# Two projection tiles and one pool of four tiles in the key phase of a linear-attention kernel with an MLP behind it

## The chip, the cores and the metric

The kernel runs on one core of one Trainium2 chip. The core has five engines with queues of their own: TensorE (PE, with its weight loads shown as PEld), VectorE (DVE), ScalarE (ACT), GpSimd (POOL) and SyncE (SP), which here issues all DMAs. The metric is the device time of one execution in microseconds (us). Before the change three runs took 1204.83, 1207.55 and 1209.04 us; the median is 1207.55 us.

## The reference

The inputs are q, k and v of 8 batches, 8 heads, 576 tokens and 64 dimensions, a feature matrix w_phi of 64x128, and the two matrices of an MLP. Everything is float32.

```python
def phi(x):
    proj = np.einsum('bhsd,df->bhsf', x, w_phi)
    proj = proj - np.max(np.abs(proj), axis=-1, keepdims=True)
    return np.concatenate([np.exp(proj), np.exp(-proj)], axis=-1)
q_p, k_p = (phi(q), phi(k))
kv = np.einsum('bhsf,bhsd->bhfd', k_p, v)
z = np.sum(k_p, axis=2)
num = np.einsum('bhsf,bhfd->bhsd', q_p, kv)
den = np.einsum('bhsf,bhf->bhs', q_p, z)[..., None] + 1e-06
return (num / den).astype(np.float32)
...
h = x @ w_in
g = np.maximum(0.01 * h, h)
return (g @ w_out).astype(np.float32)
```

The second part takes the attention output, reordered to 4608 tokens of 512 features, through w_in (512x2048) and w_out (2048x512).

## The kernel before

**Attention.** The 64 pairs of batch and head are taken two heads at a time: 32 phases i, four per batch. A key phase, k_phase(i), builds kv and z of its two heads; a query phase, q_phase(i), uses them and writes the divided result into a ring that holds two batches. Phases 0 to 3 have their own code (first_k_phase, first_q_phase) and run at the start.

**Key phase.** 576 tokens are five chunks (four of 128 and one of 64) in three groups (2, 2 and 1 chunks). For each group the projection goes from PE into a PSUM tile of tag "a", is copied by ACT and added to by DVE into `pmk` (lines 244 to 249), and DVE takes its maximum into `m4` and the negative into `m4n` (lines 252 to 256). For each chunk ACT writes four exponentials into `ek` (lines 269, 270); ACT or DVE rounds it to `kph` (helper line 67 or 69); POOL or DVE subtracts to get the remainder `kpl` (helper line 72); and PE accumulates kph and kpl against the values into a PSUM tile of tag "c" (line 224). The last chunk keeps both halves in one tile (line 289). Then the sum is copied to `kvs`, transposed (line 301) and written as `kvh` and `kvl` (lines 311 to 314). Tiles of one name share a fixed number of places: ek 1, pmk 1, kph 2, kpl 1, m4 2; "a" has 3 places, "c" has 1. A tile waits until its place is free.

**Phases below 8** ("nat") multiply in plain float32 with `bd`, two copies of w_phi on a block diagonal (lines 342, 237). **From phase 8 on** operands are split into a rounded part and a remainder, and the projections use `wq` (lines 244, 344, 345), the split of w_phi, which split_w_phi makes at the start (lines 149 to 154).

**Query phase.** Four projections into tag "a", each transposed by DVE into `tq` (line 346), a maximum into `m` (line 348), three small DMAs to bring partitions together (line 350), a second maximum `mx` (line 353), three small DMAs back (line 355), subtraction (line 361), transpose into `mb` (line 363), exponentials `eq` (lines 368, 369), rounded part `qh` (line 375) and remainder `ql` (helper line 72, POOL), matmuls with kvh and kvl (lines 384 to 389) in tag "a", copies into the ring and `dn` (lines 391, 392) and the division.

**Order.** attention() takes one step (up to a yield) of k_phase(i) and one of q_phase(i-1) in turn. All attention work has a higher priority than the MLP's; a planner turns priorities and dependencies into one fixed order for each engine, which then runs as written.

**MLP.** 18 blocks of 256 tokens. split() makes `xh` and `xl` of a block from the ring; layer1 (lines 571 to 578) and layer2 (lines 591 to 593) run for 16 steps, with `gh` and `gl` in between. Block 2 needs attention batch 1 (phases 4 to 7), block 4 needs batch 2 (phases 8 to 11), block 6 needs batch 3 (phases 12 to 15). Weights are unpacked at the start through a scratch tile that shares the place of `kvl` (line 178). The output of a block goes through tile `o` to a DMA.

Of the kernel before, what the change touches and what calls it, by code (L numbers as in the profile page):

```python
# [17 lines left out]
P = 128  # L18
# [14 lines left out]
BUFS = {"kph": 2, "eq": 2, "m4": 2, "g": 2, "gh": 2, "gl": 2, "qh": 2, "ql": 2, "dn": 2}  # L33
# [11 lines left out]
def attention_moe_kernel(ctx: ExitStack, tc: tile.TileContext, q, k, v, vt, w_phi, w_in, w_out, out):  # L45
# [8 lines left out]
    def st(shape, dt, tag):  # L54
        return sp.tile(shape, dt, tag=tag, name=tag, bufs=BUFS.get(tag, 1))

# [35 lines left out]
    wq = ct([P, 2, F], F32R, "wq")  # L92
    wq_h, wq_l = wq[:, 0], wq[:, 1]
    bd = ct([P, 2 * F], F32, "bd")
# [53 lines left out]

    def split_w_phi():
        for j in range(2):  # L150
            r = slice(64 * j, 64 * j + 64)
            w = bd[r, F * j : F * j + F]
            nc.scalar.copy(wq_h[r], w)
            nc.vector.tensor_tensor(wq_l[r], w, wq_h[r].bitcast(F32), op=ALU.subtract)
# [50 lines left out]
    def k_phase(i):  # L205
# [14 lines left out]
        yield  # L220
        kvp = pt("c")
# [5 lines left out]
        for g in range(3):  # L227
# [4 lines left out]
            pmk = st([P, 4, F], F32, "pmk")  # L232
            if nat:
# [19 lines left out]
            mb = m4[r, 0 : 2 * w].unsqueeze(2).broadcast_to([n, 2 * w, F])  # L253
            if not nat:
                m4n = st([P, 4], F32, "m4n")
                nc.vector.tensor_scalar(m4n[r, 0 : 2 * w], m4[r, 0 : 2 * w], -1.0, None, op0=ALU.mult)
            if nat:
                nc.vector.tensor_tensor(pmk[r, 0 : 2 * w], pkv, mb, op=ALU.subtract)
            yield
            for s in range(w):  # L260
                c = 2 * g + s
                ek = st([P, 2, 256], F32, ("ek", "kph", "kpl")[c % 3] if nat else "ek")
                if nat:
                    nc.scalar.activation(ek[r, :, 0:F], pmk[r, 2 * s : 2 * s + 2], AF.Exp)
                    nc.scalar.activation(ek[r, :, F:256], pmk[r, 2 * s : 2 * s + 2], AF.Exp, scale=-1.0)
                else:
                    for j in range(2):
                        h = 2 * s + j
                        nc.scalar.activation(ek[r, j, 0:F], pmk[r, h], AF.Exp, bias=m4n[r, h : h + 1])  # L269
                        nc.scalar.activation(ek[r, j, F:256], pmk[r, h], AF.Exp, scale=-1.0, bias=m4[r, h : h + 1])  # L270
                if nat:
                    for j in range(2):
                        kv_mm(j, rv[r, 4 * j + c if c < 4 else 8 + j], ek[r, j], first=c == 0, last=c == 4)
                    yield
                    continue
                if c < 4:
                    kph = st([P, 2, 256], F32R, "kph")
                    kpl = st([P, 2, 256], F32R, "kpl")
                    copy_("kph", kph, ek)
                    tt_("kpl", kpl, ek, kph.bitcast(F32), ALU.subtract)  # L280
                    for j in range(2):
                        kv_mm(j, vh[:, 4 * j + c], kph[:, j], first=c == 0)
                        kv_mm(j, vl[:, 4 * j + c], kph[:, j])
                    for j in range(2):
                        kv_mm(j, vh[:, 4 * j + c], kpl[:, j])
                else:
                    kst = st([P, 2, 256], F32R, "kph")
                    copy_("kst", kst[r], ek[r])
                    nc.vector.tensor_tensor(kst[0:64], ek[r], kst[r].bitcast(F32), op=ALU.subtract)
                    for j in range(2):  # L290
                        kv_mm(j, vl[:, 8 + j], kst[:, j])
                        kv_mm(j, vh[:, 8 + j], kst[:, j], last=True)
                yield
        kvs = st([P, 2, 256], F32, "ek").rearrange("p a (b f) -> p a b f", b=2)[0:66]
# [26 lines left out]
    def q_phase(i):  # L321
# [11 lines left out]
        yield  # L333
        tq = st([P, 2, 2, U], F32, "tq")
        m = st([P, 4, 2, 18], F32, "m")
# [75 lines left out]
    def first_k_phase(i):  # L411
# [6 lines left out]
        for g in range(3):  # L418
# [10 lines left out]
            pm = st([P, 4, F], F32, ("kpl" if g % 2 else "kph") if od else ("ek" if g % 2 else "pmk"))  # L429
# [14 lines left out]
        kvs = st([P, 2, 256], F32, "kph").rearrange("p a (b f) -> p a b f", b=2)[0:66]  # L444
# [28 lines left out]
    def first_q_phase(u):  # L473
# [7 lines left out]
        for hp in range(1 if tail else NP):  # L481
# [6 lines left out]
            pm = st([P, 4, F], F32, "ek" if hp % 2 else "pmk")  # L488
# [49 lines left out]
    def attention():  # L538
        for i in range(NP, B * NP + 1):
            gens = [k_phase(i)] if i < B * NP else []  # L540
            if i > NP:
                gens.append(q_phase(i - 1))
            while gens:
                for it in list(gens):
                    if next(it, end) is end:
                        gens.remove(it)
                    else:
                        yield i - 1
            yield i
# [33 lines left out]
    def layer2(i, ft, half=range(TT)):  # L583
# [10 lines left out]
        if ft == NFT - 1:  # L594
            for t in half:
                o = st([P, DM], F32, "ek" if i == NBLK - 1 and t else "o")
                copy_("o", o, accs[i, t])
                r = i * T + t * P
                nc.sync.dma_start(out[r : r + P, :], o)
# [27 lines left out]
    split_w_phi()  # L627
# [60 lines left out]
```

## Time and profile before

| | |
|---|---|
| three runs, median (range) | 1207.55 us (1204.83 to 1209.04) |
| the profiled execution, its time | 1207.22 us |
| the profiled execution, its span | 1205.4 us |
| busy ACT, DVE, POOL | 861.8, 747.7, 631.5 us |
| mean granted clock of TensorE | 0.992 |

The span counts from the first to the last instruction that the profile shows. A busy time is the union of an engine's instructions; matmuls overlap, and their ends are modelled, so a busy PE is not yet a PE at its peak. In the slices of the span the engines look like this (each digit is the share of a slice of about 30 us in tenths):

```profile
PE   8899999899998999899999999999999999999998
DVE  5979984566767675766677666767876767510000
ACT  5977875778787787777787877778777788543232
POOL 0042222456566676666666666656566766453232
```

Until about 210 us the start phases, the weights and the nat phases run; then attention and MLP run side by side; from about 1070 us only the MLP is left. A row of the groups gives line, engine, operation, tiles, shapes and count, then busy us and mean ns; idle time before it and what ended it stand last. The chain of work is followed back from the end, each piece to what released it.

### The profile page before, as it was taken

What the parts mean: (1) busy time and instruction counts of PE and PEld (TensorE: products, weight loads), DVE (VectorE), ACT (ScalarE), POOL (GpSimd) and SP (SyncE); (2) the same over time, 40 slices, a digit from 0 to 9 for tenths busy, and PEclk for the clock granted to TensorE, in tenths of its full rate; (3) what the DMA queues carried; (4) which work ended last, traced back from release to release, by engine and by line L of the source; (5) the groups of instructions that cost most, each with busy time, mean ns of one, the idle gap of its engine ahead of it and who ended that gap; (6) DMA issues with size and microseconds to landing.
All of it is one profiled execution on the core that took longest, in us unless ns stands there. A gap on an engine that the chain in (4) does not pass through costs nothing.

```text
span 1205.4 us, 21633 instructions
## 1 busy us (share of the span) xinstructions
PE 1168.8 (97%) x7496; PEld 1035.9 (86%) x7496; DVE 747.7 (62%) x1327; ACT 861.8 (71%) x2267; POOL 631.5 (52%) x709
## 2 busy tenths in 40 slices
PE   8899999899998999899999999999999999999998
PEld 5577778699997999799998999899989999989997
DVE  5979984566767675766677666767876767510000
ACT  5977875778787787777787877778777788543232
POOL 0042222456566676666666666656566766453232
PEclk9999999899998999899999999999999999999999
DMA  7425241201111011111111011111011110000000
GB/s 215 142 81 167 88 116 32 77 23 33 50 32 48 18 44 33 50 24 32 50 32 40 22 50 33 40 33 50 21 40 32 41 33 19 3 18 5 14 18 18
DMA packets 70846, 57.82 MB, mean 48 GB/s; under 512 B 53201, under 2 KB 54353, under 8 KB 70737
## 3 DMA queue, kind: packets, MB, share of 16 engines
q1 hardware_dynamic: 70736, 56.44, 16.6%
q8 instruction: 59, 0.97, 0.3%
q14 instruction: 51, 0.41, 0.1%
HBM read 46.20 MB, written 9.44 MB: 46 GB/s over the span
## 4 chain that ended last, share of the span: by engine, by line
PE 69%; DVE 10%; ACT 9%; issue 4%; DMA 4%; SPq 2%; POOL 2%; DVEq 0%; POOLq 0%; ACTq 0%
PE h L571 9%; PE h L574 9%; PE h L572 9%; PE acc L591 8%; PE acc L592 8%; PE acc L593 8%; PE c L224 5%; PE a L384 2%; DMA mx<-mx 2%; PE a L244 2%; PE a L389 2%; PE a L386 2%; DMA m<-m 2%; DVE tq L361 1%; SPq L350 1%
## 5 line engine op out<-in xcount | busy, mean ns | idle before, releaser
L72 POOL TENSOR_TENSOR gl<-g,gh 128x256 fp32r<-128x256 f32 x288 | 231.3, 806 | 327.9 <-ACT gh L67 259.9
L571 PE MATMUL h<-xh,w0h 128*128 128x256 f32 x1088 | 281.1, 285 | 4.4 <-ACT g L578 2.4
L572 PE MATMUL h<-xh,w0l 128*128 128x256 f32 x1088 | 277.5, 282 | 0.0
L571 PEld LDWEIGHTS h<-xh,w0h 128*128 128x128 f32 x1088 | 205.9, 189 | 18.3 <-ACT g L578 4.2
L591 PE MATMUL acc<-w1h,gh 128*128 128x512 f32 x544 | 215.3, 396 | 0.7 <-DVE o L69 0.4
L592 PE MATMUL acc<-w1l,gh 128*128 128x512 f32 x544 | 214.8, 395 | 0.0
L572 PEld LDWEIGHTS h<-xh,w0l 128*128 128x128 f32 x1088 | 205.8, 189 | 8.9
L593 PE MATMUL acc<-w1h,gl 128*128 128x512 f32 x544 | 203.4, 395 | 0.7 <-POOL gl L72 0.7
L578 ACT ACTIVATE g<-h 128x256 f32<-128x256 f32 x288 | 109.1, 381 | 110.4 <-PE h L574 85.4
L574 PE MATMUL h<-xl,w0h 128*128 128x256 f32 x1088 | 187.4, 281 | 0.0
L72 POOL TENSOR_TENSOR ql<-eq,qh 128x576 fp32r<-128x576 f32 x96 | 148.8, 1569 | 53.6 <-DVE qh L375 31.7
L67 ACT CAST gh<-g 128x256 fp32r<-128x256 f32 x288 | 114.8, 403 | 57.5 <-PE acc L592 55.1
L574 PEld LDWEIGHTS h<-xl,w0h 128*128 128x128 f32 x1088 | 154.6, 188 | 0.6 <-POOL xl L72 0.2
L72 POOL TENSOR_TENSOR kpl<-ek,kph 128x512 fp32r<-128x512 f32 x72 | 98.4, 1366 | 37.4 <-ACT kph L67 14.5
L591 PEld LDWEIGHTS acc<-w1h,gh 128*128 128x128 f32 x544 | 102.4, 188 | 14.1 <-DVE o L69 0.7
L593 PEld LDWEIGHTS acc<-w1h,gl 128*128 128x128 f32 x544 | 99.1, 188 | 17.6 <-POOL gl L72 0.9
L592 PEld LDWEIGHTS acc<-w1l,gh 128*128 128x128 f32 x544 | 102.3, 188 | 12.6
L361 DVE TENSOR_TENSOR tq<-tq,mx 128x576 f32<-128x576 f32 x56 | 59.2, 1097 | 80.3 <-DMA mx<-mx 80.3
L269 ACT ACTIVATE ek<-pmk,m4n 128x128 f32<-128x128 f32 (+1 forms) x240 | 89.8, 393 | 16.1 <-POOL kpl L72 12.6
L375 DVE TENSOR_REDUCE qh<-eq 128x576 fp32r<-128x576 f32 x96 | 70.8, 749 | 44.4 <-ACT eq L369 20.2
L270 ACT ACTIVATE ek<-pmk,m 128x128 f32<-128x128 f32 (+1 forms) x240 | 89.1, 390 | 8.6 <-DVE m L252 8.1
L368 ACT ACTIVATE eq<-mb 128x288 f32<-128x288 f32 x112 | 49.2, 439 | 53.5 <-DVE mb L363 50.1
(202 smaller groups left out, 2363.9 us busy)
## 6 DMA issues: line engine op xcount, KB each, us to landing
out_dram<-o SPq DMA_DIRECT2D x35, 256.0 KB, 2.0
rq<-in_q_dram SPq DMA_DIRECT2D x28, 288.0 KB, 3.0
rk<-in_k_dram SPq DMA_DIRECT2D x27, 288.0 KB, 2.8
rv<-in_v_dram SPq DMA_DIRECT2D x29, 256.0 KB, 3.6
ring<-in_w_in_dram SPq DMA_DIRECT2D x9, 512.0 KB, 3.8
f<-in_w_out_dram SPq DMA_DIRECT2D x7, 512.0 KB, 3.6
f<-in_w_in_dram SPq DMA_DIRECT2D x7, 512.0 KB, 3.7
ring<-in_w_out_dram SPq DMA_DIRECT2D x5, 512.0 KB, 3.8
```

The lines of the kernel that those rows point to most:

```text
L67: nc.scalar.copy(o, i)
L72: (nc.vector if pick(key) == "v" else nc.gpsimd).tensor_tensor(o, a, b, op=op)
L269: nc.scalar.activation(ek[r, j, 0:F], pmk[r, h], AF.Exp, bias=m4n[r, h : h + 1])
L270: nc.scalar.activation(ek[r, j, F:256], pmk[r, h], AF.Exp, scale=-1.0, bias=m4[r, h : h + 1])
L361: nc.vector.tensor_tensor(tu, tu, mx[:, u].unsqueeze(2).broadcast_to([P, 18, 32]), op=ALU.subtract)
L571: nc.tensor.matmul(ph, lhsT=weight(0, "h", ft)[:, d * P : d * P + P], rhs=xh[d], start=d == 0, stop=False)
L572: nc.tensor.matmul(ph, lhsT=weight(0, "l", ft)[:, d * P : d * P + P], rhs=xh[d], start=False, stop=False)
L574: nc.tensor.matmul(ph, lhsT=weight(0, "h", ft)[:, d * P : d * P + P], rhs=xl[d], start=False, stop=d == NP - 1)
L578: nc.scalar.activation(g, ph, AF.Prelu, alpha=0.01)
L591: nc.tensor.matmul(a, lhsT=gh[:, ts], rhs=weight(1, "h", ft), start=ft == 0, stop=False)
L592: nc.tensor.matmul(a, lhsT=gh[:, ts], rhs=weight(1, "l", ft), start=False, stop=False)
L593: nc.tensor.matmul(a, lhsT=gl[:, ts], rhs=weight(1, "h", ft), start=False, stop=ft == NFT - 1)
```

## The change

The tiles ek, kph, kpl and kvs of the key phase get one common tag "kk" with four places (before 1 + 2 + 1). pmk gets two places, m4 three and m4n two. k_phase is cut into head(g), the projection and maximum of a group, and chunk(c); the program order becomes head 0, chunk 0, head 1, chunk 1, head 2, chunks 2 to 4, where it was head 0, chunks 0 and 1, head 1, chunks 2 and 3, head 2, chunk 4. The arithmetic is the same.

The places come from three others: wq now takes the place of bd, so it is made when phase 8 first asks for it (w_phi_split), from a second load of w_phi into the place of kvl; the query's m takes the place of mb. In attention(), q_phase(7) is taken five steps ahead of k_phase(8), since it is the last to read bd.

```diff
@@ -30,7 +30,7 @@
 NK = 8
-BUFS = {"kph": 2, "eq": 2, "m4": 2, "g": 2, "gh": 2, "gl": 2, "qh": 2, "ql": 2, "dn": 2}
+BUFS = {"kk": 4, "pmk": 2, "eq": 2, "m4": 3, "m4n": 2, "g": 2, "gh": 2, "gl": 2, "qh": 2, "ql": 2, "dn": 2}
 PBUFS = {"a": 3, "c": 1, "h": 2, "acc": 2}
@@ -51,8 +51,8 @@
 
-    def st(shape, dt, tag):
-        return sp.tile(shape, dt, tag=tag, name=tag, bufs=BUFS.get(tag, 1))
+    def st(shape, dt, tag, name=None):
+        return sp.tile(shape, dt, tag=tag, name=name or tag, bufs=BUFS.get(tag, 1))
 
@@ -89,9 +89,19 @@
     xl = ct([P, NP, T], F32R, "xl")
-    wq = ct([P, 2, F], F32R, "wq")
-    wq_h, wq_l = wq[:, 0], wq[:, 1]
-    bd = ct([P, 2 * F], F32, "bd")
+    bd = cp.tile([P, 2 * F], F32, tag="bd", name="bd", bufs=1)
+    split_w = {}
+
+    def w_phi_split():
+        if not split_w:
+            raw = st([P, F], F32, "kvl", "wr")
+            for j in range(2):
+                nc.sync.dma_start(raw[64 * j : 64 * j + 64], w_phi)
+            split_w[0] = w = cp.tile([P, 2, F], F32R, tag="bd", name="wq", bufs=1)
+            nc.scalar.copy(w[:, 0], raw)
+            nc.vector.tensor_tensor(w[:, 1], raw, w[:, 0].bitcast(F32), op=ALU.subtract)
+        return split_w[0]
+
     xbh = [st([P, 2, U], F32R, "qh")[:, :, 0:T] for _ in range(2)]
@@ -145,13 +155,6 @@
         first_load_v(i)
-
-    def split_w_phi():
-        for j in range(2):
-            r = slice(64 * j, 64 * j + 64)
-            w = bd[r, F * j : F * j + F]
-            nc.scalar.copy(wq_h[r], w)
-            nc.vector.tensor_tensor(wq_l[r], w, wq_h[r].bitcast(F32), op=ALU.subtract)
 
@@ -218,18 +221,22 @@
         yield
+        wq = None if nat else w_phi_split()
         kvp = pt("c")
...
 
-        for g in range(3):
+        heads = {}
+
+        def head(g):
             w = 2 if g < 2 else 1
...
             pmk = st([P, 4, F], F32, "pmk")
+            m4n = None
             if nat:
@@ -250,48 +257,58 @@
             nc.vector.tensor_reduce(m4[r, 0 : 2 * w], pkv, axis=AX.X, op=ALU.max, apply_absolute_value=True)
-            mb = m4[r, 0 : 2 * w].unsqueeze(2).broadcast_to([n, 2 * w, F])
-            if not nat:
+            if nat:
+                mb = m4[r, 0 : 2 * w].unsqueeze(2).broadcast_to([n, 2 * w, F])
+                nc.vector.tensor_tensor(pmk[r, 0 : 2 * w], pkv, mb, op=ALU.subtract)
+            else:
                 m4n = st([P, 4], F32, "m4n")
                 nc.vector.tensor_scalar(m4n[r, 0 : 2 * w], m4[r, 0 : 2 * w], -1.0, None, op0=ALU.mult)
+            heads[g] = r, pmk, m4, m4n
+            yield
+
+        def chunk(c):
+            g, s = divmod(c, 2)
+            r, pmk, m4, m4n = heads[g]
+            ek = st([P, 2, 256], F32, "kk", "ek")
             if nat:
-                nc.vector.tensor_tensor(pmk[r, 0 : 2 * w], pkv, mb, op=ALU.subtract)
-            yield
-            for s in range(w):
-                c = 2 * g + s
-                ek = st([P, 2, 256], F32, ("ek", "kph", "kpl")[c % 3] if nat else "ek")
-                if nat:
-                    nc.scalar.activation(ek[r, :, 0:F], pmk[r, 2 * s : 2 * s + 2], AF.Exp)
-                    nc.scalar.activation(ek[r, :, F:256], pmk[r, 2 * s : 2 * s + 2], AF.Exp, scale=-1.0)
-                else:
-                    for j in range(2):
-                        h = 2 * s + j
-                        nc.scalar.activation(ek[r, j, 0:F], pmk[r, h], AF.Exp, bias=m4n[r, h : h + 1])
-                        nc.scalar.activation(ek[r, j, F:256], pmk[r, h], AF.Exp, scale=-1.0, bias=m4[r, h : h + 1])
-                if nat:
-                    for j in range(2):
-                        kv_mm(j, rv[r, 4 * j + c if c < 4 else 8 + j], ek[r, j], first=c == 0, last=c == 4)
-                    yield
-                    continue
-                if c < 4:
-                    kph = st([P, 2, 256], F32R, "kph")
-                    kpl = st([P, 2, 256], F32R, "kpl")
-                    copy_("kph", kph, ek)
-                    tt_("kpl", kpl, ek, kph.bitcast(F32), ALU.subtract)
-                    for j in range(2):
-                        kv_mm(j, vh[:, 4 * j + c], kph[:, j], first=c == 0)
-                        kv_mm(j, vl[:, 4 * j + c], kph[:, j])
-                    for j in range(2):
-                        kv_mm(j, vh[:, 4 * j + c], kpl[:, j])
-                else:
-                    kst = st([P, 2, 256], F32R, "kph")
-                    copy_("kst", kst[r], ek[r])
-                    nc.vector.tensor_tensor(kst[0:64], ek[r], kst[r].bitcast(F32), op=ALU.subtract)
-                    for j in range(2):
-                        kv_mm(j, vl[:, 8 + j], kst[:, j])
-                        kv_mm(j, vh[:, 8 + j], kst[:, j], last=True)
-                yield
-        kvs = st([P, 2, 256], F32, "ek").rearrange("p a (b f) -> p a b f", b=2)[0:66]
+                nc.scalar.activation(ek[r, :, 0:F], pmk[r, 2 * s : 2 * s + 2], AF.Exp)
+                nc.scalar.activation(ek[r, :, F:256], pmk[r, 2 * s : 2 * s + 2], AF.Exp, scale=-1.0)
+                for j in range(2):
+                    kv_mm(j, rv[r, 4 * j + c if c < 4 else 8 + j], ek[r, j], first=c == 0, last=c == 4)
+                return
+            for j in range(2):
+                h = 2 * s + j
+                nc.scalar.activation(ek[r, j, 0:F], pmk[r, h], AF.Exp, bias=m4n[r, h : h + 1])
+                nc.scalar.activation(ek[r, j, F:256], pmk[r, h], AF.Exp, scale=-1.0, bias=m4[r, h : h + 1])
+            if c < 4:
+                kph = st([P, 2, 256], F32R, "kk", "kph")
+                kpl = st([P, 2, 256], F32R, "kk", "kpl")
+                copy_("kph", kph, ek)
+                tt_("kpl", kpl, ek, kph.bitcast(F32), ALU.subtract)
+                for j in range(2):
+                    kv_mm(j, vh[:, 4 * j + c], kph[:, j], first=c == 0)
+                    kv_mm(j, vl[:, 4 * j + c], kph[:, j])
+                for j in range(2):
+                    kv_mm(j, vh[:, 4 * j + c], kpl[:, j])
+            else:
+                kst = st([P, 2, 256], F32R, "kk", "kst")
+                copy_("kst", kst[r], ek[r])
+                nc.vector.tensor_tensor(kst[0:64], ek[r], kst[r].bitcast(F32), op=ALU.subtract)
+                for j in range(2):
+                    kv_mm(j, vl[:, 8 + j], kst[:, j])
+                    kv_mm(j, vh[:, 8 + j], kst[:, j], last=True)
+
+        yield from head(0)
+        chunk(0)
+        yield
+        yield from head(1)
+        chunk(1)
+        yield
+        yield from head(2)
+        for c in range(2, 5):
+            chunk(c)
+            yield
+        kvs = st([P, 2, 256], F32, "kk", "kvs").rearrange("p a (b f) -> p a b f", b=2)[0:66]
         copy_("kvs", kvs, kvp[0:66].rearrange("p (a b f) -> p a b f", a=2, b=2))
@@ -331,8 +348,11 @@
         yield
+        if not nat:
+            wq = w_phi_split()
+            wq_h, wq_l = wq[:, 0], wq[:, 1]
         tq = st([P, 2, 2, U], F32, "tq")
-        m = st([P, 4, 2, 18], F32, "m")
+        m = st([P, 4, 2, 18], F32, "mb", "m")
         for u in range(2):
@@ -426,7 +446,7 @@
             nc.vector.tensor_reduce(m4[r, 0 : 2 * w], pkv, axis=AX.X, op=ALU.max, apply_absolute_value=True)
-            pm = st([P, 4, F], F32, ("kpl" if g % 2 else "kph") if od else ("ek" if g % 2 else "pmk"))
+            pm = st([P, 4, F], F32, "kk" if od else "pmk", "pm")
             nc.vector.tensor_tensor(pm[r, 0 : 2 * w], pkv,
@@ -441,7 +461,7 @@
                 yield
-        kvs = st([P, 2, 256], F32, "kph").rearrange("p a (b f) -> p a b f", b=2)[0:66]
+        kvs = st([P, 2, 256], F32, "kk", "kvs").rearrange("p a (b f) -> p a b f", b=2)[0:66]
         copy_("kvs", kvs, kvp[0:66].rearrange("p (a b f) -> p a b f", a=2, b=2))
@@ -485,7 +505,7 @@
             nc.vector.tensor_reduce(m4[0:n, 0 : 2 * ns], pqv, axis=AX.X, op=ALU.max, apply_absolute_value=True)
-            pm = st([P, 4, F], F32, "ek" if hp % 2 else "pmk")
+            pm = st([P, 4, F], F32, "kk" if hp % 2 else "pmk", "pm")
             nc.vector.tensor_tensor(pm[0:n, 0 : 2 * ns], pqv,
@@ -540,6 +560,10 @@
                 gens.append(q_phase(i - 1))
+            if i == NN:
+                for _ in range(5):
+                    next(gens[1])
+                    yield i - 1
             while gens:
@@ -593,7 +617,7 @@
             for t in half:
-                o = st([P, DM], F32, "ek" if i == NBLK - 1 and t else "o")
+                o = st([P, DM], F32, "kk" if i == NBLK - 1 and t else "o", "o")
                 copy_("o", o, accs[i, t])
@@ -624,7 +648,6 @@
     together(first_q_phase(2))
-    split_w_phi()
     for t in range(TT):
```

## The prediction

> **Times.** The profiled execution took 1207.2 us, 1.8 us more than its span of 1205.4 us. The median of the three runs, 1207.55 us, lies 0.3 us above it. The sum is made on 1207.2. The measurement tells 0.3% (3.6 us) from no change.
>
> **What bounds the kernel now.** First the head of the page, then the busy time by stretches (columns: stretch, length, PE, PEld, DVE, ACT, POOL busy with counts, granted clock, DMA share, GB/s).
>
> ```profile
> span 1205.4 us, 21633 instructions
> PE 1168.8 (97%) x7496; PEld 1035.9 (86%) x7496; DVE 747.7 (62%) x1327; ACT 861.8 (71%) x2267; POOL 631.5 (52%) x709
> 210.00:240.00 30.00, 25.62 (x130) 19.33 (x129) 15.39 (x27) 21.57 (x60) 12.65 (x20) 0.89 0.26 77
> 360.00:390.00 30.00, 25.85 (x157) 22.93 (x156) 22.85 (x42) 21.55 (x57) 19.97 (x20) 0.89 0.13 39
> 480.00:510.00 30.00, 24.70 (x148) 21.63 (x148) 21.82 (x39) 23.54 (x66) 18.92 (x23) 0.94 0.17 46
> 510.00:540.00 30.00, 29.66 (x202) 27.76 (x202) 20.06 (x38) 23.18 (x63) 19.30 (x21) 0.95 0.11 26
> 520.00:1050.00 530.00, 526.42 (x3594) 484.31 (x3593) 363.12 (x623) 412.61 (x1117) 338.24 (x357) 1.00 0.12 34
> ```
>
> TensorE is the bound: from 520 to 1050 us it is busy 526.42 of 530 us at clock 1.00, and there a faster key phase buys nothing. Three places are open, where the MLP waits for a batch of attention to finish. There PE idles and then runs below full clock. Idle plus lost clock: 210 to 240, 4.38 + 0.11 x 30 = 7.7 us; 360 to 390, 4.15 + 3.3 = 7.5 us; 480 to 540, 5.30 + 0.34 + 0.06 x 30 + 0.05 x 30 = 8.9 us. Together 24.1 us.
>
> What ends those waits is read from the chain of work, asked for two stretches (start, length, what).
>
> ```profile
> 341.81 0.44 DVE pmk L249
> ...
> 343.23 0.69 ACT ek L270 x2
> 344.77 0.70 ACT ek L269 x2
> ...
> 345.95 0.40 DVE kph L289
> ...
> 347.18 0.43 DVE pmk L249
> 347.66 0.40 PE a L344
> ...
> 355.20 1.73 DMA m<-m
> ...
> 358.64 2.53 DMA mx<-mx
> ...
> 363.31 0.66 DVE pmk L249 x2
> ...
> 370.56 1.53 POOL kpl L72
> ...
> 379.32 0.39 PE h L571
> ```
>
> From 347.66 on this is query phase 11, the last of batch 2: projection, two DMA round trips, exponentials, division into the ring, the split (xh), and the MLP matmul that had waited. Ahead of it stands key phase 11: group 2's projection (pmk at 341.81), then its chunk 4 (the two pairs of ek, then kph), then key phase 12's first pmk (347.18), and only then the projection of the query. The second pmk cannot be written before chunk 4 has read the first, since there is one tile. Two more pieces of key work sit inside the query's own chain: pmk, 0.66 us on DVE, and kpl, 1.53 us on POOL.
>
> **The change part by part.**
>
> *Second pmk, heads early.* Instruction counts stay the same: the exponentials, casts and subtractions per phase are those of before, so nothing is saved but waiting. How long does a projection wait for its pmk?
>
> ```profile
> 308.76 0.29 PE L244 MATMUL a<-wq,ks 128*128 128x256 f32 x1
> ...
> 312.17 0.37 ACT L67 COPY pmk<-a 128x256 f32<-128x256 f32 x1
> ...
> 722.23 0.39 PE L244 MATMUL a<-wq,ks 128*128 128x256 f32 x2
> 723.25 0.37 ACT L67 COPY pmk<-a 128x256 f32<-128x256 f32 x1
> ```
>
> In the first case the projection ends at 309.05 and its copy begins at 312.17, 3.1 us later; between them ACT works off chunk 4's exponentials, which still read the old pmk; in the second the wait is 723.25 - 722.62 = 0.6 us. The query's projections share PSUM tag "a" with these tiles and inherit the wait. The mean of the two cases is 1.9 us per phase; I take 1.6, since the copy needs some delay anyway. Bounds: 0, where the query chain paces the phases by itself, and 5.9 us, the stretch 341.81 to 347.66 of the chain; it is nearest to what the two cases show. Each stall ends four phases (8 to 11, 12 to 15), so 4 x 1.6 = 6.4 us of the 7.5 and of the 8.9: 12.8, I write 13. Late next are the two DMA trips, which do not change, and then PE itself.
>
> *Pool kk of four.* ek (1), kph (2) and kpl (1) become four shared tiles: no memory, no instruction. A chunk's exponentials can run beside the last chunk's kpl.
>
> ```profile
> ACT ek L269 <- POOL kpl L72: 12.6, 15, 1.5
> ```
>
> These waits are 12.6 us in the whole kernel (the view of waits: us, times, longest), 0.5 us for each of 24 key phases. MLP matmuls of PE's queue hide them wherever no block waits. I add nothing for it beside the 1.6. Where the pool is short, since kvs now holds one of the four as it held ek, a chunk waits as before; I bound this by the same 0.5 us a phase, 2 us a batch, in both directions.
>
> *Query phase 7 ahead of key phase 8.* Five steps of q_phase(7) now come first, so its four projections no longer alternate with key tiles.
>
> ```profile
> L346 DVE STREAM_TRANSPOSE tq<-a 128x288 f32<-128x288 f32 x112 | 51.3, 469 | 19.6 <-PE a L345 15.6 <-PE a L342 3.2
> ...
> 207.74 0.68 PE a L342 x2
> ...
> 211.66 0.68 PE a L342 x2
> ...
> 215.33 0.74 PE a L342 x4
> ...
> 216.94 0.76 DVE m L348
> ```
>
> A row with x2 is one tile here. Two tiles with nothing between them took 0.74 us (the x4 row); four need about 1.5 us, and their transposes (L346, 0.47 us each) run behind them, the last ending near 207.74 + 0.7 + 4 x 0.47 = 210.3 us with some slack to 211. The maximum (m) could start near 211 us in place of 216.94, up to 6 us earlier, and this chain ends the stall at 210 to 240. Bounds 0 and 6; I take 5 of the 7.7 us, near the upper one, since all that follows in that chain stays as it is.
>
> *w_phi loaded again.*
>
> ```profile
> bd<-in_w_phi_dram SPq DMA_DIRECT2D x2, 32.0 KB, 3.0
> L179 ACT ACTIVATE kvl<-qs x4: 662/665/669, 150.6 to 180.0; 128x512 int32<-128x512 uint32 x4
> L386 PE MATMUL a<-qh,kvl x192: 290/295/445, 265.5 to 1062.1; 128*128 128x288 f32 x192
> L314 DVE TENSOR_TENSOR kvl<-c,kvh x24: 407/415/415, 252.3 to 1045.0; 128x256 fp32r<-128x256 f32 x24
> L244 PE MATMUL a<-wq,ks x240: 275/280/644, 206.4 to 1025.1; 128*128 128x256 f32 x120
> L106 POOL MEMSET vhl<- x1: 117/117/117, 221.0 to 221.0; 128x20 f32 x1
> ```
>
> Two DMAs of 32 KB (3.0 us to landing) go through SP's queue, ahead of m transfers and k, q loads; one copy and one subtraction of 128x128, bounded by the 0.29 us of the old 64x128 forms and the 0.40 us of L249, replace two of each at the start. The raw tile shares kvl's place, which the weights use last at 180.0 + 0.7 us, so it lands near 185. If it could take that place before the weights it would block them for 200 us; the tile vhl speaks against it, since its memset waits for nothing but its place and still ran at 221.0, after its predecessor's last use. The split tile then waits for bd, which query phase 7 reads last, about 211 us (216 if the step before fails). Key phase 8's first projection moves from 206.4 to about 212, 6 us, at worst 11. Behind the copy wait ACT's exponentials and casts, behind the subtraction DVE's. The cover: key phase 8 delivers kvl at 252.3 + 0.4 us and the query uses it first at 265.5, 12.8 us of slack. Cost 0; without cover, up to 11 us in the stall at 360.
>
> *m in mb's place.* A query's maximum must wait for the exponentials on the last mb.
>
> ```profile
> 353.27 0.67 DVE m L348
> 335.28 0.43 ACT L369 ACTIVATE eq<-mb 128x288 f32<-128x288 f32 x1
> ```
>
> The last exponentials of query phase 10 ended at 335.71. Phase 11's second m began at 353.27, and its first cannot start before its projection at 347.66: 12 us of cover, cost 0.
>
> **The sum.** 1207.2 - 5 - 13 = 1189.2, forecast **1189 us**. The Trainium skill, "Perfetto Trace Analysis", section "Identifying the Most-Contended Engine", judges TensorE by its weight loads and not by matmul busy time. With 484.31 of 530 us (91.4%) as the full rate, the stretches above lack 8.1, 4.5 and 5.4 us, 18.0 in place of my 24.1; by the same shares (18 of 24.1) the gain would be 13.4 and the time 1194 us.
>
> **Rivals.**
>
> *A. The query chain paces.* From 355 to 379 us the chain is query work nearly alone, DMA trips included. If key work only rode along, the phases keep their pace and only phase 7's reorder gains, 0 to 5 us: 1202 to 1207, in the middle **1204.7 us**. For it: those rows. Against: the stretch from 341.81 to 347.66, where key work holds the query's projection.
>
> *B. Key work in the query's way (slower).* Heads and chunks that run earlier meet the query's subtraction (L361) on DVE and its ql on POOL.
>
> ```profile
> 668.88 2.83 DVE L361 TENSOR_TENSOR tq<-tq,mx 128x576 f32<-128x576 f32 x2 [3.15 <-DMA mx<-mx]
> 669.64 1.45 POOL L72 TENSOR_TENSOR kpl<-ek,kph 128x512 fp32r<-128x512 f32 x1 [0.32 <-PE c L224]
> 704.86 1.43 DVE L361 TENSOR_TENSOR tq<-tq,mx 128x576 f32<-128x576 f32 x2 [3.09 <-DMA mx<-mx]
> L361 DVE TENSOR_TENSOR tq<-tq,mx 128x576 f32<-128x576 f32 x56 | 59.2, 1097 | 80.3 <-DMA mx<-mx 80.3
> ```
>
> Beside a kpl the pair took 2.83 us, alone 1.43; the mean pair takes 2.19, so at most 0.64 us more per phase. One more kpl in front of a ql adds 1.45. Together 2.1 us per phase, 8.4 per batch, two stalls 16.8: **1224 us**; with half of it 1216. It decides from the point where such delays exceed the 1.6 us that the second pmk frees. The Trainium skill, "SBUF — State Buffer", section "Who interferes with whom", has the rule: a VectorE instruction with two SBUF inputs and a GpSimd instruction that reads SBUF exclude each other, the second waiting for the first; the trace agrees (2.83 against 1.43 us). If by it every phase met one kpl, the 0.64 us would make 2.6 us a batch and 5 us in all, 1194 us.
>
> *C. w_phi late.* Key phase 8 slips by 11 us and uses up the slack: 1207.2 + 11 = **1218 us**. The 12.8 us of slack speak against it.
>
> **How the numbers follow.** Forecast 0.60, A 0.21, B 0.13, C 0.06. The forecast's own range is 1180 to 1200: 24.1 us and some small idle gone at the low end (1207.2 - 24.1 - 3.6 = 1179.5, the last term the idle of 520 to 1050), 7 us gained at the other. The range 1180 to 1214 takes in A and the milder part of B, leaving out most of B and C. Faster by over 0.3%: the forecast 0.60 and half of A, 0.70. Within: half of A and the mildest of B, 0.13. Slower: 0.17.
>
> **What would show it.** Right: the stretches near 235, 365 and 500 at clock 1.00 with PE busy over 29 of 30 us; pmk copies within 1 us of their projection; the four L342 pairs within 2 us; L314's 24 instances starting about where they did but closer together up to 515 us; 520 to 1050 as full as before. Wrong: stalls as long at the same blocks (A), L361 pairs over 2.2 us in the mean or ql behind kpl in the chain (B), L386 first used after 275 us (C). A schedule that differs in places that I did not look at, the first 90 us above all, could move the time by some us either way.

## The result, and the profile after

The changed kernel takes **1188.89 us** (median of four runs, 1187.88 to 1190.31), beside 1208.3 us of the kernel before (median of four, the three above and 1209.08); the ratio is 0.9843, 95% interval 0.9824 to 0.9862. Forecast were 1189 us and 1180 to 1214. The profiled execution took 1187.94 us.

The head of the page of the kernel after, then its busy time by stretches (stretch, length, PE, PEld, DVE, ACT, POOL busy with counts, granted clock, DMA share, GB/s):

```profile
span 1186.2 us, 21604 instructions
PE 1153.7 (97%) x7496; PEld 1026.5 (87%) x7496; DVE 769.2 (65%) x1326; ACT 861.3 (73%) x2266; POOL 632.7 (53%) x709
```

```profile
210.00:240.00 30.00, 26.07 (x168) 22.47 (x168) 19.59 (x36) 25.64 (x73) 16.88 (x23) 1.00 0.23 68
360.00:390.00 30.00, 26.83 (x184) 23.87 (x185) 25.48 (x45) 27.03 (x74) 20.57 (x21) 1.00 0.18 50
480.00:510.00 30.00, 28.81 (x196) 26.16 (x195) 22.80 (x38) 22.91 (x66) 19.64 (x26) 1.00 0.16 47
510.00:540.00 30.00, 29.03 (x198) 26.04 (x198) 20.79 (x36) 22.73 (x63) 19.72 (x20) 1.00 0.09 22
520.00:1050.00 530.00, 526.33 (x3597) 485.64 (x3598) 361.53 (x617) 411.58 (x1115) 344.61 (x366) 1.00 0.12 32
```

The span is 19.2 us shorter, and it can be split in three. Idle PE: 1205.4 - 1168.8 = 36.6 us before, 1186.2 - 1153.7 = 32.5 after, **4.1 us**. The same 7496 matmuls keep PE busy 15.1 us less. Most of that is clock: its mean was 0.992 and is 1.000 (0.997 to 0.999 in the other three runs of the kernel after), 0.008 x 1205.4 = **9.6 us**; all four stretches that stood at 0.89 to 0.95 are at 1.00. What is left, **5.5 us**, belongs to no stall and was not in the forecast. By the measure of the prediction (idle and lost clock in the three stalls) 3.9 + 3.2 + 2.2 = 9.3 us remain of 24.1: 14.8 gained, 18 forecast.

The 5.5 us show where only the MLP is left. The last four matmuls of layer 1, six MLP steps apart, in PE's timeline (start, us, engine, line, operation), kernel before, then after:

```profile
1133.02 0.64 PE L574 MATMUL h<-xl,w0h 128*128 128x256 f32 x4
...
1149.95 0.64 PE L574 MATMUL h<-xl,w0h 128*128 128x256 f32 x4
```

```profile
1114.50 0.64 PE L598 MATMUL h<-xl,w0h 128*128 128x256 f32 x4
...
1131.30 0.64 PE L598 MATMUL h<-xl,w0h 128*128 128x256 f32 x4
```

16.93 and 16.80 us: 2.82 us a step before, 2.80 after. There are 18 x 16 = 288 such steps, so 0.022 x 288 = some 6 us, although these lines of code are the same in both kernels.

Where did the rest come from? A key phase ends with kvl. Its rows by line (count, duration in ns, first and last start), cut to key phases 8 to 16, before and after:

```profile
L314 DVE TENSOR_TENSOR kvl<-c,kvh x9: 412/415/415, 252.3 to 526.6; 128x256 fp32r<-128x256 f32 x9
```

```profile
L331 DVE TENSOR_TENSOR kvl<-c,kvh x9: 407/414/417, 250.2 to 496.7; 128x256 fp32r<-128x256 f32 x9
```

Eight key phases took 274.3 us, 34.3 each; they take 246.5, **30.8 each**. The attention that the three stalls wait for ends with the last division into the ring. These rows are from POOL's timeline, before (batches 1, 2, 3), then after:

```profile
243.11 0.80 POOL L72 TENSOR_TENSOR ring<-ring,dn 128x288 f32<-128x288 f32 x1 [1.85 <-DVE dn L399]
...
379.25 0.98 POOL L72 TENSOR_TENSOR ring<-ring,dn 128x288 f32<-128x288 f32 x1 [1.99 <-DVE dn L399]
...
515.63 0.97 POOL L72 TENSOR_TENSOR ring<-ring,dn 128x288 f32<-128x288 f32 x1 [1.93 <-DVE dn L399]
```

```profile
236.80 0.80 POOL L72 TENSOR_TENSOR ring<-ring,dn 128x288 f32<-128x288 f32 x1 [4.69 <-DVE dn L419]
...
374.98 0.81 POOL L72 TENSOR_TENSOR ring<-ring,dn 128x288 f32<-128x288 f32 x1 [0.45 <-DVE dn L419]
...
499.90 0.82 POOL L72 TENSOR_TENSOR ring<-ring,dn 128x288 f32<-128x288 f32 x1 [0.54 <-PE acc L617]
```

By these starts batch 1 is done 6.3 us earlier, batch 2 4.3, batch 3 15.7. What shrank is a cadence, not one chain at each stall.

### The profile page after: what moved, and what is told of

Read it like the earlier page. It is cut to its first block, busy times and chain, and to the rows that moved or that the text cites. A ratio compares the mean times of both kernels' runs of the same rounds, so it can differ in the third digit from the quotient of the medians.

```text
span 1186.2 us, 21604 instructions
## 1 busy us (share of the span) xinstructions
PE 1153.7 (97%) x7496; PEld 1026.5 (87%) x7496; DVE 769.2 (65%) x1326; ACT 861.3 (73%) x2266; POOL 632.7 (53%) x709
## 4 chain that ended last, share of the span: by engine, by line
PE 47%; DVE 2%; DMA 1%; issue 0%; ACT 0%; POOL 0%; SPq 0%; DVEq 0%; ACTq 0%; POOLq 0%
PE h L598 6%; PE h L596 6%; PE h L595 6%; PE acc L616 6%; PE acc L617 6%; PE acc L615 6%; PE c L228 3%; PE a L409 1%; PE a L404 1%; PE a L406 1%; PE a L251 1%; PE a L365 1%; PE a L364 1%; DVE tq L381 0%; DMA mx<-mx 0%
## 5 line engine op out<-in xcount | busy, mean ns | idle before, releaser
L72 POOL TENSOR_TENSOR gl<-g,gh 128x256 fp32r<-128x256 f32 x288 | 237.3, 827 | 305.4 <-ACT gh L67 220.2
L598 PE MATMUL h<-xl,w0h 128*128 128x256 f32 x1088 | 191.2, 281 | 0.0
L72 POOL TENSOR_TENSOR ql<-eq,qh 128x576 fp32r<-128x576 f32 x96 | 142.9, 1500 | 53.3 <-DVE qh L395 44.3
L72 POOL TENSOR_TENSOR kpl<-ek,kph 128x512 fp32r<-128x512 f32 x72 | 101.5, 1410 | 75.9 <-ACT kph L67 59.3
L69 DVE COPY o<-acc 128x512 f32<-128x512 f32 x17 | 11.7, 688 | 161.0 <-DMA out_dram<-o 118.0
L256 DVE TENSOR_TENSOR pmk<-a,pmk 128x256 f32<-128x256 f32 (+1 forms) x120 | 49.6, 420 | 54.0 <-ACT pmk L67 52.0
```

What stands on the lines that cost most here:

```text
L72: (nc.vector if pick(key) == "v" else nc.gpsimd).tensor_tensor(o, a, b, op=op)
L598: nc.tensor.matmul(ph, lhsT=weight(0, "h", ft)[:, d * P : d * P + P], rhs=xl[d], start=False, stop=d == NP - 1)
```

## The experiments

My theory at this point was that of the prediction: query chains end the stalls, the second pmk and the early heads speed them up, the pool is free of effect. The rival: **key phases pace everything**, and whatever shortens one counts. Each run below is set against the kernel before on the same chip (1208.3 to 1209.2 us). The pace is that of key phases 8 to 16, worked out as above from the nine kvl rows of each trace.

| kernel | us | ratio, 95% interval | us per key phase |
|---|---|---|---|
| after | 1188.89 | 0.9843, 0.9824 to 0.9862 | 30.8 |
| e1, phase 7 first, in the kernel before | 1215.45 | 1.0053, 1.0035 to 1.0071 | 34.3 |
| e2, one pmk | 1194.71 | 0.9882, 0.9869 to 0.9895 | 31.1 |
| e3, old order | 1193.42 | 0.9872, 0.9856 to 0.9889 | 32.2 |
| e4, own tiles | 1197.72 | 0.9911, 0.9897 to 0.9925 | 31.8 |
| e5, pool alone of the three | 1196.01 | 0.9902, 0.9890 to 0.9915 | 32.1 |
| e6, none of the three | 1206.45 | 0.9975, 0.9963 to 0.9987 | 34.0 |
| e7, one pmk, phase 7 in lockstep | 1193.61 | 0.9882, 0.9866 to 0.9898 | 31.3 |
| e8, own tiles, two for exponentials | 1195.30 | 0.9891, 0.9878 to 0.9903 | 31.5 |
| e11, query step first | 1182.25 | 0.9778, 0.9761 to 0.9795 | 30.6 |
| e12, query step first, in the kernel before | 1214.46 | 1.0058, 1.0037 to 1.0078 | 34.8 |

The pace tells the kernels over 1206 us (34.0 to 34.8) from those under 1198 (30.6 to 32.2). Among the faster ones it does not give the order: e3 at 32.2 is no slower than e8 at 31.5.

### Each of the three parts taken out

One projection tile (e2), heads and chunks in the order of before (e3), own tiles in place of the pool (e4):

```diff
-BUFS = {"kk": 4, "pmk": 2, ...
+BUFS = {"kk": 4, "pmk": 1, ...
```

```diff
-        chunk(0)
-        yield
+        for c in range(2):
+            chunk(c)
+            yield
         yield from head(1)
...
```

```diff
-            ek = st([P, 2, 256], F32, "kk", "ek")
+            ek = st([P, 2, 256], F32, ("ek", "kph", "kpl")[c % 3] if nat else "ek", "ek")
...
-                kph = st([P, 2, 256], F32R, "kk", "kph")
-                kpl = st([P, 2, 256], F32R, "kk", "kpl")
+                kph = st([P, 2, 256], F32R, "kph")
+                kpl = st([P, 2, 256], F32R, "kpl")
...
```

> The kernel after with one place for pmk. My theory (the second pmk frees the projections, 13 us): most of the gain is lost, 1200 to 1203 us (ratio 0.994 to 0.996), waits of projections for pmk come back to several us, and the stall at 480 to 540 returns to about 9 us. Rival (order of the program or the pool did it): 1189 to 1193 us (ratio 0.984 to 0.988).

> The kernel after with the old program order of heads and chunks (chunk 1 ahead of head 1, chunk 3 ahead of head 2), two pmk and the pool kept. My theory: the second pmk does the work whatever the order, 1189 to 1194 us (ratio 0.984 to 0.988). Rival (the order does it, since it puts the last key projection ahead of the query's matmuls in the shared PSUM places): 1198 to 1203 us (ratio 0.992 to 0.996).

> The kernel after with places of their own for ek (1), kph (2) and kpl (1) in place of the pool of four. My theory: the pool is worth at most 2 us a batch of phases at two stalls, 1189 to 1193 us (ratio 0.984 to 0.988). Rival (the pool, which lets exponentials run beside the last remainder, does it): 1198 to 1203 us (ratio 0.992 to 0.996).

By the ratios the second tile is worth 0.0039 x 1209 = 4.7 us, the order 0.0029, 3.5 us, and the pool 0.0068, **8.2 us**; the intervals leave each of these uncertain by 2 to 3 us. The part that I had costed at nothing is the largest. The run with one tile lies between my theory and its rival, and its stretch of 480 to 540 lacks 1.0 us, not 9; the old order came out as my theory had it, the own tiles close to the rival (0.9911 against 0.992). One row that the pool removes stands in the view of waits of e4 (us, times, longest):

```profile
ACT ek L281 <- POOL kpl L72: 13.9, 21, 1.6
```

ACT waits there for GpSimd to finish reading the only exponential tile. In the kernel before it was 12.6 us; in the kernel after there is no such row. Other rows changed with it, so this one is not yet the price of the pool.

### Do the parts add?

e5 is e2 and e3 together, e6 takes e4 as well.

> The changed kernel with one projection tile in place of two and the old order of heads and chunks; of the three parts of the key phase only the pool of four is left, beside the early query phase 7 and the reloaded w_phi. Theory 1, the parts add: 1188.9 + 4.7 (second tile, from the run with one) + 3.5 (order, from the run with the old order) = 1197 us, ratio 0.990. Theory 2, the pool pays only beside a second projection tile or the new order, which let a chunk's exponentials start while the last kpl runs: most of its 8 us is gone here, 1203 us, ratio 0.995.

> The changed kernel without all three parts of the key phase: own tiles for exponentials (1), rounded values (2) and remainders (1), one projection tile, old order; left are the early query phase 7, the reloaded w_phi and the maximum in mb's place. Theory 1, the parts add: 1188.9 + 4.7 + 3.5 + 8.2 = 1205 us, ratio 0.997. Theory 2, each of the three removes the same wait in the end, and where two are gone the third has nothing left to lose: 1198 to 1200 us, ratio 0.992. Theory 3, the reordered query phase 7 costs here as it did alone in the kernel before (1.0053): 1213 to 1216 us.

They add: 1197 expected and 1196.01 measured, 1205 and 1206.45. The pool by itself is worth 0.9975 - 0.9902 = 0.0073 of 1209, 8.8 us (1206.45 - 1196.01 = 10.4 by the medians), close to its share beside the other two. The three sum to 16.4 us, where e6 and the change differ by 0.0132 x 1209 = 16.0. So, within the noise of 2 to 3 us, no part merely enables another.

### What of the pool?

e8 has e4's tiles in other numbers, the same memory:

```diff
-BUFS = {"kph": 2, "pmk": 2, ...
+BUFS = {"ek": 2, "pmk": 2, ...
```

> As the run with tiles of their own (1197.7 us), but two tiles for the exponentials, one for rounded values, one for remainders, in place of 1, 2, 1: same memory, no pool. Theory 1, the pool pays because ACT need not wait for GpSimd's kpl to read the only exponential tile (13.9 us of waits in the run with own tiles): 1189 to 1191 us, ratio 0.984, and those waits gone. Theory 2, the pool pays by sharing, since any of the four serves whichever comes next, a second rounded tile among them: 1195 to 1198 us, ratio 0.990, with ACT or DVE waiting for the matmuls that read the one rounded tile.

The time is that of theory 2: by the medians a second exponential tile is worth 2.4 of the 8.8 us between e4 and the change. The old wait went down, another went up, and the wait that theory 2 named, for matmuls that read the one rounded tile, is the last of these rows. e8:

```profile
POOL kpl L72 <- ACT kph L67: 84.5, 31, 5.3
ACT ek L281 <- POOL kpl L72: 5.0, 12, 1.1
ACT kph L67 <- PE c L228: 0.9, 3, 0.3
```

POOL waits 84.5 us for the rounded value, which now has one place, against 59.3 us in the kernel after and 65.9 in e4. But POOL's wait alone is no cost: in the kernel before it was 14.5 us. And e8 takes a place from the rounded values as it gives one to the exponentials, so its 2.4 us is a balance of the two and prices neither wait. The runs show that two fixed shares of the four tiles, 1, 2, 1 and 2, 1, 1, are worse than the common tag. That the tag pays by giving the free tile to whoever comes next is my reading and not shown.

### Query phase 7 first

e1 adds this part alone to the kernel before; e7 takes it from e2 (wq finds a place of its own where the second pmk was, so bd need not be free). With both projection tiles there is no memory for that, so e7 speaks for one projection tile alone.

```diff
             if i > NP:
                 gens.append(q_phase(i - 1))
+            if i == NN:
+                for _ in range(5):
+                    next(gens[1])
+                    yield i - 1
```

> The kernel before with only query phase 7's five early steps. My theory (5 us of the gain come from here): the maximum of query phase 7 starts near 211 us in place of 216.9, the stall at 210 to 240 shrinks, and the time falls by 3 to 5 us, to about 1203 to 1205 us (ratio 0.996 to 0.998). Rival (all of the gain is key work): no change, 1208 us.

> The changed kernel with one projection tile, with w_phi's split tile at a place of its own (the memory of the second projection tile pays for it) and with query phase 7 in lockstep with key phase 8 as before; to be set against the run with one projection tile, 1194.7 us, which differs by the early phase 7 and the place alone. My prediction's step, that the early phase 7 takes 5 us from the stall at 210 to 240: 1199 to 1200 us here, ratio 0.992, query phase 7's maximum about 5 us later. Rival, that it delays key phase 8 and costs what it cost alone: 1188 to 1190 us, ratio 0.983. Third, that it does nothing once key phases run freely: 1194 to 1196 us.

Alone it makes the kernel **slower** by 0.5%, against my step that gave it 5 us. The second maximum of query phase 7 starts at 215.56 us, 1.4 us earlier than before and not near 211, and the last division of batch 1 no earlier (243.87 us, before 243.11). The stretches and kvl rows of e1:

```profile
210.00:240.00 30.00, 24.98 (x142) 19.62 (x141) 15.89 (x27) 19.73 (x54) 12.54 (x21) 1.00 0.23 67
360.00:390.00 30.00, 18.18 (x86) 14.48 (x85) 21.80 (x39) 20.30 (x56) 12.39 (x11) 0.72 0.18 49
L314 DVE TENSOR_TENSOR kvl<-c,kvh x9: 407/415/416, 260.1 to 534.5; 128x256 fp32r<-128x256 f32 x9
```

Key phase 8 ends 7.8 us later (252.3 to 260.1), the pace stays at 34.3, so all later phases are late, batch 2 ends 8.3 us later, and the stall at 360 grows to 11.8 us idle at clock 0.72. Where key phases run faster (e7 against e2) it does nothing that can be told: 1193.61 without, 1194.71 with, both at 0.9882.

### Who paces? The same edit on both kernels

e12 and e11 put the query's step ahead of the key's in every turn, in the kernel before and after:

```diff
+            gens.reverse()
             while gens:
                 for it in list(gens):
```

> The changed kernel, where in every turn of the lockstep the query phase's step stands ahead of the key phase's (before: behind it). Theory 1, what is left of the three stalls (3.9, 3.2 and 2.2 us) still ends on the query chain, which key work holds up: 2 to 4 us gained, 1185 to 1187 us, ratio 0.982. Theory 2, the chain is paced by the key phases that deliver the next query's weights, as in the run with the early phase 7 on the kernel before: key work that stands behind comes later, 1191 to 1196 us, ratio 0.988. Theory 3, the order within a turn does not matter: 1188 to 1190 us.

> The kernel before with the query phase's step ahead of the key phase's in every turn of the lockstep, none of the change in it. Set against the same edit on the changed kernel, which took 6.6 us off (1188.9 to 1182.25). Theory 1, the query chain paces both kernels, and key work only stands in its way: 4 to 9 us gained here too, 1200 to 1205 us, ratio 0.994. Theory 2, in the kernel before the key phases pace, with one projection tile and one exponential tile, and putting them behind the query delays the next query's weights, as with query phase 7 alone (1.0053): 1212 to 1218 us, ratio 1.005.

Opposite signs: 6.6 us gained on the kernel after, more than any theory had forecast, and 5.9 lost on the kernel before (by the medians; by the ratios 7.9 and 7.0). e12's kvl rows, and the ends of its batches 1 and 2:

```profile
L314 DVE TENSOR_TENSOR kvl<-c,kvh x9: 405/414/414, 248.4 to 526.8; 128x256 fp32r<-128x256 f32 x9
```

```profile
231.91 0.79 POOL L72 TENSOR_TENSOR ring<-ring,dn 128x288 f32<-128x288 f32 x1
...
379.33 0.81 POOL L72 TENSOR_TENSOR ring<-ring,dn 128x288 f32<-128x288 f32 x1 [1.92 <-DVE dn L399]
```

Batch 1 is done 11 us earlier than before (232.7 against 243.9), and batch 2 at the same moment (380.1 against 380.2): key phases at 34.8 us each have eaten the lead. Where the loss shows is the stall at batch 2, in e12's stretches:

```profile
330.00:360.00 30.00, 25.44 (x164) 21.83 (x162) 18.65 (x36) 23.82 (x65) 20.94 (x25) 0.94 0.16 41
360.00:390.00 30.00, 24.27 (x140) 21.65 (x141) 23.65 (x39) 21.86 (x58) 14.18 (x15) 0.77 0.11 31
```

The MLP comes there earlier and finds batch 2 no earlier: PE idles 10.3 us of the 60, in the kernel before 4.4, and the clock is lower. So from batch 2 on the query chain did not pace the kernel before. What fits is the key phases: the three parts of the change that shorten them shorten the time too. In the kernel after a smaller lead lasts longer. The ends of e11's batches 1 and 2:

```profile
232.38 0.81 POOL L72 TENSOR_TENSOR ring<-ring,dn 128x288 f32<-128x288 f32 x1 [1.18 <-DVE dn L419]
...
369.82 0.82 POOL L72 TENSOR_TENSOR ring<-ring,dn 128x288 f32<-128x288 f32 x1
```

That is 4.4 and 5.2 us earlier than in the kernel after, and batch 3 is 0.8 us earlier. There the query chain is worth going first: e11 is faster than both kernels, 1182.25 us. Its key phases come no later for it (30.6 us each), so that they never limit the kernel after is not shown.

### The shorter MLP step

Two kernels only move addresses, with every engine's order kept. e9: the kernel before with wq behind the weights, which so lie 1024 bytes lower, as in the kernel after. e10: the kernel after, 32 bytes higher.

```diff
-    wq = ct([P, 2, F], F32R, "wq")
+    wq = st([P, 2, F], F32R, "wq")
```

```diff
-    ring = ct([P, 2, NP, S], F32, "ring")
+    gap, ring = ct([P, 8], F32, "gap"), ct([P, 2, NP, S], F32, "ring")
```

> The kernel before with one edit: the split w_phi (1 KB per partition) is allocated behind the MLP's weights in place of ahead of them, so that all weight tiles lie 1024 bytes lower, as in the changed kernel; every engine's order of instructions is that of the kernel before. Theory 1, the shorter distance between starts of 512-wide matmuls in the changed kernel (lower quartile 227 ns, in the kernel before 230 ns) comes from where the weights lie: it appears here too, and 1727 such matmuls x 2 to 3 ns make 3.5 to 5 us, 1204 to 1205.5 us, ratio 0.9965. Theory 2, it comes from something else that changed (the schedule, the queues): 1209 us, ratio 1.000, lower quartile 230 ns.

> The changed kernel with 32 unused bytes ahead of everything but the identity, so that the weight tiles lie 32 bytes higher (82944 in place of 82912, a whole multiple of 1024); order of instructions as in the changed kernel. Theory 1, the place of the weights modulo some power of two sets the distance of the 512-wide matmuls: it moves by 1 ns or more, up or down, and the time by 2 us or more from 1188.9 us. Theory 2, only the 1024 bytes mattered, or nothing of the place does: 1188 to 1190 us, ratio 0.984.

e9 took 1207.41 us (0.9988, 0.9976 to 1.0001), e10 1190.98 (0.9850, 0.9833 to 0.9867). The place of the weights, as far as these two moves go, is not it. In the trace records the last 700 matmuls, from first start to last, take 110.89 us in the kernel before, e1, e9 and e12, and 109.95 us in the kernel after and all kernels made from it, e6, e7 and e10 too. Most of it lies in layer 2: there the starts of its 512-wide matmuls are 231.9 ns apart in the mean before and in e9, 228.6 after and in e10. What of the rewritten part (the reload, the places of m and of the small tiles, the queue that results) makes the step shorter stays **open**.

## Why the prediction was right, point by point

The time was right to 0.1 us; its terms were not, so the closeness is luck.

**What bounds the kernel.** PE and the three stalls: right, and 520 to 1050 is as full as before. That query chains with key work in their way end the stalls is true of the chain that the prediction followed, but the pace of the key phases decided when those chains could start. The chain of waits from 341.81 to 347.66 was a piece of that pace, and I read it as an obstacle to the query.

**Second pmk, heads early, 13 us.** Right in kind, too large: 4.7 + 3.5 = 8.2 us. In this case the wait went as foreseen; the projection in PE's timeline and its copy in ACT's, kernel after:

```profile
304.94 0.40 PE L251 MATMUL a<-wq,ks 128*128 128x256 f32 x2
305.37 0.37 ACT L67 COPY pmk<-a 128x256 f32<-128x256 f32 x1 [0.17 <-PE a L251]
```

0.03 us in place of 3.1. Over all 120 copies (the n-th copy against the end of the n-th pair of projection matmuls) the mean wait was 4.91 us before and is 1.15 us after, with 54 copies still over 1 us. The mean of 1.9 us that the prediction took came from two cases and was too small. Nor does this wait give the price of the part: its mean is 4.02 us in e2 and 2.08 in e5, and e5 is not the faster.

**The pool, nothing, 2 us a batch at most.** This is the step that failed most: 8.2 us beside the others, 8.8 alone. That MLP matmuls hide such waits was beside the point: the pool shortened the key phase, by 1.0 us from e4 to the change and 1.9 from e6 to e5, and nothing hid a longer key phase from the blocks that waited for it. The row of waits that I priced held 0.5 us a phase and cannot be the whole of that; which waits carry the rest stays open.

**Query phase 7, 5 us.** Failed: +6.4 us alone, nothing measurable with the pool. The four projections in a row were to bring the maximum 6 us forward; the new order alone brings 1.4 us (e1) or 2.4 (217.13 in e7, 214.75 in e2), and it delays key phase 8, which batch 2 needs. In the kernel after the second m starts here, in DVE's timeline:

```profile
207.28 0.74 DVE L368 TENSOR_REDUCE m<-tq 128x18 f32<-128x576 f32 x1
```

This is 9.7 us earlier than 216.94 (211 forecast), though the four projections still came in two pairs 3.7 us apart. But most of it is the work of the key phase's tiles: without the second projection tile (e2) the start is 214.75, without the pool (e4) 211.43.

**w_phi, m in mb's place, nothing.** The first key projection is at 209.1 us (212 forecast), and kvl at 250.2 has 7 us before its first use. Neither was taken out by itself; e6, which holds both, phase 7's order and the shorter MLP step, is 3.0 us faster than before by the ratio (2.3 by the medians). As the shorter MLP step alone makes some 6 us, the others together cost some 3, by this estimate, and not nothing: in e6 PE is busy 20.82 us from 360 to 390 at clock 0.72, before 25.85 at 0.89. 3.0 + 16.4 = 19.4 us closes the account with the 19 us measured.

**Rivals.** A, that the query chain paces: wrong for the kernel before (e12); in the kernel after, putting that chain first pays (e11). B, collisions with the query's subtraction: the mean is 1105 ns where it was 1097, so 2.21 us for a pair. That is just over the 2.2 us of the prediction's sign, but 0.02 us more than before, not 0.64. A ql stands right behind a kpl on POOL 5 times, before 7. So no. C: first use of kvl at 257.9 us, not after 275.

```profile
L381 DVE TENSOR_TENSOR tq<-tq,mx 128x576 f32<-128x576 f32 x56 | 59.6, 1105 | 15.7 <-DMA mx<-mx 15.1
L406 PE MATMUL a<-qh,kvl x192: 289/295/303, 257.9 to 1019.8; 128*128 128x288 f32 x192
```

The Trainium skill's measure, "Perfetto Trace Analysis", "Identifying the Most-Contended Engine", gave 1194 us. By weight loads the four stretches now lack 5.0 + 3.6 + 1.3 + 1.5 = 11.4 us against 485.64 of 530, where it was 18.0: 6.6 us gained, where the clock and the idle time say 14.8. Here it was the worse measure of what a stall costs, since it does not see the slower clock as a loss: in the row of 366 to 369 us below the weight loads are busy 2.70 of 3 us at a clock of 0.53.

**The signs.** Clock 1.00 in the stretches of the stalls, kvl closer together and 520 to 1050 as full as before came true. PE busy over 29 of 30 us did not (26.07, 26.83 and 28.81), nor did the copies within 1 us and the projections within 2 us.

So 13 + 0 + 5 stands against 8.2 + 8.2 + 3.0, and the 3.0 is a shorter MLP step that was not in the forecast, less what the rest cost: the right total by errors that cancelled, the pool too small, the other two too large.

## What to carry to other kernels

Ask which chain sets the pace over many turns, not which one ended last at a stall: a microsecond or two on the pacing chain counts in every turn, and here a lead won elsewhere was eaten before the next stall. An edit that puts one side first is a cheap test: here it lost time where the other side paced and gained once that side was faster, so it is worth repeating after each change of the pace. Where several short-lived tiles of one size follow each other, try one pool: here it beat both fixed shares of the same memory that were run, by 6.4 and 8.8 us.

## What the runs showed of the hardware

Of the 14.8 us gained at the stalls, 9.9 were clock (0.11 x 30 twice, 0.06 and 0.05 x 30). At 366 us what cost clock was a short stretch of thin work, without any long gap. Kernel before:

```profile
363.00:366.00 3.00, 1.10 (x5) 0.38 (x3) 2.90 (x7) 1.31 (x4) 1.43 (x1) 1.00 0.00 0
366.00:369.00 3.00, 2.70 (x11) 2.70 (x12) 1.80 (x4) 2.67 (x8) 2.67 (x2) 0.53 0.23 87
```

PE busy 1.10 of 3 us, with no single gap over 1.4 us in the records, and the next 3 us run at 0.53. In the kernel after, of the four slices of 3 us from 360 to 372, the thinnest has PE busy 1.66, and the clock stays:

```profile
360.00:363.00 3.00, 1.66 (x8) 0.99 (x8) 2.48 (x3) 2.90 (x8) 2.72 (x2) 1.00 0.00 0
363.00:366.00 3.00, 2.12 (x16) 1.85 (x16) 2.70 (x6) 2.71 (x6) 1.80 (x2) 1.00 0.23 87
```

These two cases give no threshold. In e11 a slice that was fuller than this one, with no gap over 0.6 us, was followed by a low clock:

```profile
360.00:363.00 3.00, 1.87 (x12) 1.34 (x10) 1.38 (x5) 2.40 (x7) 2.84 (x4) 1.00 0.23 87
363.00:366.00 3.00, 2.64 (x13) 2.40 (x13) 2.61 (x7) 0.67 (x3) 0.78 (x3) 0.55 0.63 166
```

The Trainium skill, "TensorE: Matmul & The Clock Gate", section "Why this matters for your kernels", asks for no idle gap over some 3 us; in the stretch at 366 us of the kernel before the clock fell without one. Filling a stall part of the way can thus save more than the idle time that it fills: here 9.9 us of clock beside 4.9 of idle time.
